# Stores of the last batch from SP's and ScalarE's queues, a three-part store as three operations, and a new order of all engines

## The chip, the cores and the metric

The kernel runs on one core of a Trainium2 chip. The metric is the device time of one execution in microseconds (us). The engines are PE (TensorE, matrix products), VectorE (DVE), ScalarE (ACT), GpSimd (POOL) and SyncE (SP). Each works through its own list of instructions in order and waits on semaphores for the others. DMAs are issued from the lists of SP, POOL and, after the change, ScalarE.

## The reference

Attention over blocks mixed by a Sinkhorn-normalized matrix, then a Fourier mix and a feed-forward layer, over 4 batches, 768 tokens and 8 heads of 64 (so 512 columns):

```python
for _ in range(5):
    P = P - np.max(P, axis=-1, keepdims=True)
    P = np.exp(P)
    P = P / (np.sum(P, axis=-1, keepdims=True) + 1e-09)
    P = P / (np.sum(P, axis=-2, keepdims=True) + 1e-09)
k_sorted = np.einsum('bhij,bhjcd->bhicd', P, k_b)
v_sorted = np.einsum('bhij,bhjcd->bhicd', P, v_b)
scores = scale * np.matmul(q_b, k_sb.transpose(0, 1, 2, 4, 3))
attn = softmax(scores);  x = attn @ v_sb      # x: (4, 768, 512)
...
mixed = np.real(fft(fft(x, axis=1), axis=2))
u = x + mixed
un = (u - mu) / np.sqrt(var + 1e-06)
ch = np.maximum(un @ w_ch1, 0.0) @ w_ch2      # 512 -> 2048 -> 512
out = u + ch                                  # float32
```

## The kernel before

The 768 tokens of a batch are handled as six tiles of 128 rows. `TOK` lists the tokens of each: tiles T = 0, 1, 2 hold tokens 1 to 383 and token 0 at the end of T = 2, tiles T = 3, 4, 5 the mirrored tokens downward from 767. A row of T = 0, 1 lies beside the next one in the output, so those tiles are stored by one plain DMA. T = 2 is stored in three parts: 112 rows, 15 rows and the single row of token 0. T = 3, 4, 5 run backwards in the output and are stored by POOL with an indirect DMA over a table of row numbers (`rows`, line 1627).

Per batch the work is: block mixing of k and v (`kq`, `vmix`), transposes of q, scores, exponentials on ScalarE (line 1268), subtraction of 1 (`em1`, line 1281 on VectorE or 1283 on ScalarE), the product with v (`av`, line 1298), the division (line 1315), two DFT steps (`dft1`, `dft2`), the normalization (square, logarithm L1534, exponential, `un`), a transpose (`uT`, `utev`), and the feed-forward layer. For batches 0 and 1 its first product is `ff1` (line 1592). For batches 2 and 3 `ff1_seven` (from line 1698 on) builds the product from seven smaller ones: VectorE forms the differences E1, a second one in place, E2 and E4 of the inputs (operations tagged `es`, line 1716); the products (line 1728) collect in banks A, D and Q; ScalarE copies A out (line 1743), VectorE adds (line 1736). The second product in batches 1 to 3 is `ff2_chunk` (line 1779 on), one chunk per pair of tiles (t, t + 3), again with sums on VectorE (line 1796), products of 8 matmuls (line 1820), a copy by ScalarE (`p1`, line 1851) and additions into u by VectorE (line 1837). A chunk's last product is `p3`; the addition behind it completes the tile T = t, which is then stored. In batch 3 the chunks are planned in the order t = 2, 0, 1, and the last one, t = 1, stores its tile in two halves of 256 columns: the left half after `p2`, the right one after `p3`.

What is issued, and in which order, is written out by hand. `P.add` collects operations, numbered in the order in which they are added, each with the engines that may do it, its cost on each, its function, what it reads and writes, and a tag. `ORDER` holds for each engine the list of these numbers. `schedule` goes through the five lists, gives out buffers and returns the order in which the instructions are emitted; it does not change the lists. An operation that names two engines is done by the one in whose list it stands. The tool that makes dependencies would order all stores to `out` behind one another; `declare_no_dep` says which pairs write different rows.

`store` (line 1609) is one operation per tile. For T = 2 it issues all three parts on SP. Its cost says SP for T < 3 and POOL for T > 2. The engine lists hold 461 (PE), 347 (ACT), 568 (DVE), 70 (POOL) and 61 (SP) numbers. In batch 3 these numbers matter below: 1331 and 1345 are products with E2, 1324 makes E2; 1488 is the first product of chunk t = 1, whose bank ScalarE copies; 1460, 1481 and 1503 are the last products (`p3`) of the chunks t = 2, 0 and 1; 1461, 1482 and 1504 the additions behind them; 1462, 1483, 1502 and 1505 the stores of T = 2, T = 0 and of the two halves of T = 1; 1498 is the addition before POOL's last store (1499, T = 4). Before the first `ff1`: 272, 275 and 278 are `un`, 273, 276 and 279 the transposes, 274, 277 and 280 the copies of those into `ut`; 394 is an attention product. The numbers are those of the kernel before; after the change all from 1463 on are higher by 2.

PE works in several kinds of matmul (full tile, halves, quarters); `MODE` and `TURN` are the planner's notion of what a change from one kind to the next costs.

Of the kernel before, what the change touches and what calls it, by code (L numbers as in the profile page):

```python
# [22 lines left out]
DM = 512  # L23
# [44 lines left out]
    ),  # L68
    "ACT": (
# [425 lines left out]
def kernel(  # L495
# [10 lines left out]
    nc = tc.nc  # L506
# [9 lines left out]
    P = Plan()  # L516
# [99 lines left out]
    def load(dst, src, nbytes, w, prio, eng="POOL", r=(), after=(), gone=()):  # L616
# [10 lines left out]
          tag="spin")  # L627
# [78 lines left out]
    for n in range(2):  # L706
# [8 lines left out]
          prio=-9100.0, tag="small")  # L715
# [76 lines left out]
    def ptb():  # L792
# [5 lines left out]
        tag="pk")  # L798
# [1233 lines left out]
```

## Time and profile before

| | before |
|---|---|
| median of 3 runs | 255.49 us (255.2 to 255.81) |
| the profiled execution | 255.66 us |
| its span, first to last instruction | 253.5 us |
| granted TensorE clock, mean | 0.996 |
| PE, VectorE, ScalarE, POOL busy | 96%, 89%, 62%, 22% |
| DMA packets | 42775, 26.51 MB |

Times inside the profile run from the span's start. A line of the instructions in order of time gives start and duration in us, the engine, the line of the kernel, the operation and its tiles; in brackets stands the engine's idle time before it and what ended it. SPq is SP's queue: the time there is the issue of a DMA, not its transfer. A line of the busy times by stage gives from:to, the length, and for each engine the busy time with the number of instructions.

### The profile page before, as it was taken

What the parts mean: (1) busy time and instruction counts of PE and PEld (TensorE: products, weight loads), DVE (VectorE), ACT (ScalarE), POOL (GpSimd) and SP (SyncE); (2) the same over time, 40 slices, a digit from 0 to 9 for tenths busy, and PEclk for the clock granted to TensorE, in tenths of its full rate; (3) what the DMA queues carried; (4) which work ended last, traced back from release to release, by engine and by line L of the source; (5) the groups of instructions that cost most, each with busy time, mean ns of one, the idle gap of its engine ahead of it and who ended that gap; (6) DMA issues with size and microseconds to landing.
All of it is one profiled execution on the core that took longest, in us unless ns stands there. A gap on an engine that the chain in (4) does not pass through costs nothing.

```text
span 253.5 us, 7235 instructions
## 1 busy us (share of the span) xinstructions
PE 244.3 (96%) x2895; PEld 167.5 (66%) x2895; DVE 226.0 (89%) x604; ACT 157.3 (62%) x372; POOL 56.2 (22%) x86
## 2 busy tenths in 40 slices
PE   4999999999999999999999999999999999999992
PEld 1347775676665666654667658887667887667882
DVE  4699999999999788989999999998889987799892
ACT  4159999999753779645886685524699425563000
POOL 8955322243359000012100000021100000310031
PEclk9999999999999999999999999999999999999998
DMA  6999999999999933033412003232202410410025
GB/s 129 206 211 314 210 214 217 208 207 184 140 133 158 189 18 75 0 79 101 83 27 48 0 5 70 50 106 83 83 3 43 65 21 0 168 43 3 0 83 207
DMA packets 42775, 26.51 MB, mean 105 GB/s; under 512 B 30202, under 2 KB 39176, under 8 KB 42740
## 3 DMA queue, kind: packets, MB, share of 16 engines
q0 software_dynamic: 23632, 18.35, 43.5%
q1 hardware_dynamic: 19110, 7.71, 15.7%
q8 instruction: 22, 0.36, 0.6%
q14 instruction: 11, 0.09, 0.1%
HBM read 29.07 MB, written 6.29 MB: 139 GB/s over the span
## 4 chain that ended last, share of the span: by engine, by line
PE 87%; DMA 5%; DVE 5%; issue 1%; POOL 1%; ACT 0%; DVEq 0%; POOLq 0%
PE bank L1820 17%; PE bank L1592 17%; PE bank L1728 14%; PE bank L1649 8%; PE bank L1298 5%; DMA kq<-in_k_dram 5%; PE bank L961 4%; PE bank L1259 3%; PE bank L1463 3%; PE bank L1372 3%; DVE u L1837 3%; PE bank L1192 1%; PE bank L1467 1%; PE bank L967 1%; PE bank L1228 1%; PE bank L1063 1%
## 5 line engine op out<-in xcount | busy, mean ns | idle before, releaser
L1592 PE MATMUL bank<-ut,w1sb 128*128 128x384 f16 x256 | 47.6, 326 | 0.0
L1268 ACT ACTIVATE ex<-bank 96x384 f32<-96x384 f32 x64 | 28.7, 486 | 11.2 <-PE bank L1451 5.6
L1627 POOL DMA_INDIRECT out_dram<-u,rows x9 | 9.8, 1094 | 114.8 <-DVE u L1837 79.2
L1743 ACT COPY vsf<-bank 128x384 f32<-128x384 f32 x48 | 21.5, 483 | 22.1 <-PE bank L1728 21.7
L1592 PEld LDWEIGHTS <-w1sb 128*128 128x128 f16 x256 | 23.5, 97 | 14.6 <-issue 0.3
L1820 PEld LDWEIGHTS <-hr 128*128 128x128 f16 x288 | 28.2, 98 | 4.3
L1736 DVE CUSTOM_DVE_ANT_0 hr<-bank,vsf 128x384 f16<-128x384 f32 x48 | 24.9, 551 | 3.1 <-PE bank L1728 2.2
L1649 PE MATMUL bank<-w2sb,hr 128*128 128x512 f16 x96 | 23.7, 379 | 0.0
L1820 PEld LDWEIGHTS <-vcx 128*128 128x128 f16 x216 | 21.1, 98 | 3.3
L1604 ACT ACTIVATE hr<-bank 128x384 f16<-128x384 f32 x41 | 19.4, 489 | 4.4 <-PE bank L1592 4.2
L1728 PE MATMUL bank<-ut,w1sb 128*128 128x384 f16 x96 | 20.9, 326 | 0.0
L1820 PE MATMUL bank<-w2sb,hr 128*128 128x256 f16 x144 | 18.2, 273 | 0.0
L1820 PE MATMUL bank<-kq,vcx 128*128 128x256 f16 x144 | 18.0, 273 | 0.0
L1298 PEld LDWEIGHTS <-eb 97*128 97x128 f16 x416 | 15.7, 98 | 3.4 <-issue 0.7
L1298 PE MATMUL bank<-vsf,eb 97*128 97x65 f16 x416 | 17.4, 193 | 0.2
L1728 PEld LDWEIGHTS <-w1sb 128*128 128x128 f16 x128 | 12.5, 98 | 7.4
L619 POOL DMA_DIRECT2D kq<-in_q_dram x18 | 15.5, 875 | 8.1 <-PE bank L1451 2.1
L1315 DVE TENSOR_TENSOR rt<-bank,rz 128x384 f16<-128x384 f32 x32 | 16.9, 547 | 0.2
L1281 DVE TENSOR_SCALAR eb<-ex 96x384 f16<-96x384 f32 x46 | 15.9, 359 | 1.2 <-ACT ex L1268 1.1
L862 ACT CAST vsf<-bank 96x512 f16<-96x512 f32 x20 | 12.9, 681 | 5.4 <-PE bank L961 5.3
L862 ACT CAST ks<-bank 128x384 f16<-128x384 f32 x24 | 10.6, 486 | 6.5 <-PE bank L1192 5.0
L1522 ACT ACTIVATE ex<-u,mv 128x512 f16<-128x512 f32 x18 | 13.0, 724 | 1.9 <-DVE mv L1514 1.6
(202 smaller groups left out, 531.5 us busy)
## 6 DMA issues: line engine op xcount, KB each, us to landing
w1sb<-in_moe_w_ch_dram POOLq DMA_DIRECT2D x4, 512.0 KB, 20.4
w2sb<-in_moe_w_ch_dram POOLq DMA_DIRECT2D x4, 512.0 KB, 22.1
hr<-in_v_dram POOLq DMA_DIRECT2D x2, 768.0 KB, 9.3
kq<-in_v_dram POOLq DMA_DIRECT2D x2, 768.0 KB, 16.6
kq<-in_k_dram POOLq DMA_DIRECT2D x8, 192.0 KB, 6.6
kq<-in_q_dram POOLq DMA_DIRECT2D x16, 96.0 KB, 6.5
out_dram<-u SPq DMA_DIRECT2D x5, 256.0 KB
kq<-in_k_dram POOLq DMA_DIRECT2D x2, 384.0 KB, 10.1
```

The lines of the kernel that those rows point to most:

```text
L862: (nc.scalar.copy if e == "ACT" else V.tensor_copy)(dst, src)
L1268: nc.scalar.activation(ex.ap[0:96], pss[h2].ap[0:96, 0:384], AF.Exp, scale=SCALE),
L1281: V.tensor_scalar(ed, src, -1.0, None, op0=ALU.add)
L1298: nc.tensor.matmul(po.ap[:, 65 * T:65 * T + 65], eb.ap[:, e0:e0 + 128], vsf[0:97, vi:vi + 65], start=(n == 0), stop=(n == len(WIN[T]) - 1) ...
L1315: P.add({"DVE": (0.465, 0.56)}, lambda _: V.tensor_tensor(rt.ap[:, :, D * h:D * h + D], po3()[:, :, 0:D], rz.ap[:, :, None].broadcast_to([ ...
L1592: nc.tensor.matmul(ps.ap[:, 0:GT], w1sb[:, c, 128 * fc:128 * fc + 128], ut.ap[:, c, :], start=(c == 0), stop=(c == 3))
L1604: nc.scalar.activation(hr[g][:, fc, :], ps.ap[:, 0:GT], AF.Relu)
L1649: nc.tensor.matmul(ps.ap, hr[g][:, fc, 128 * tt:128 * tt + 128], w2sb[:, fc, :], start=(fc == 0), stop=(fc == 15))
L1728: nc.tensor.matmul(ps.ap[:, 0:GT], lhs[:, c, fi], rhs()[:, c, :], start=(start and c == 0), stop=(c == 1), skip_group_check=True)
L1736: return P.add({"DVE": (0.47, 0.57)}, lambda _: V._custom_dve(TENSOR_ADD_SAT, out=hr[g][:, fc, :], in0=p.ap[:, 0:GT], in1=o.ap, s0=FMAX, s ...
L1743: P.add({"ACT": act(GT)}, lambda _: nc.scalar.copy(x.ap, A.ap[:, 0:GT]), r=[A], w=[x], prio=pr_v - 1, tag="pc", after=avs)
L1820: nc.tensor.matmul(ps.ap[:, o:o + 256], lhs()[:, fc], rhs[:, fc], start=(start and fc == 0), stop=(fc == 7), skip_group_check=True)
```

## The change

Three things change.

- In batch 3 the tiles T = 0, 1, 2 are stored through operations that SP or ScalarE may issue, whichever list holds them. T = 2's three parts become three operations (1462, 1463 and 1464 in the new numbering).
- The pairs of stores that are free of order are kept in one more list (`late`, for the stores issued by ScalarE).
- The lists of PE, ScalarE and VectorE are written anew, those of POOL and SP in part. 95 operations change their engine: 44 from ScalarE to VectorE, 50 from VectorE to ScalarE, and one store (the left half of T = 1, 1502 before) from SP to ScalarE, where the two new parts of T = 2 also stand. The lists of PE and POOL hold the same operations as before.

At the end of the lists the new order has, in the old numbers: PE ... 1473 1470 1488 1493 1460 1500 1481 1503; VectorE ... 1495 1496 1453 1497 1474 1461 1498 1501 1482 1504; ScalarE 1489, the single row of T = 2, 1502, the 15 rows of T = 2; SP ... 1321 1300 1279, the 112 rows of T = 2, 1483, 1505. Before, PE ended with 1500 1491 1493 1481 1449 1503 1460, VectorE with 1482 1501 1498 1453 1504 1461, ScalarE with 1489, and SP with 1321 1300 1483 1502 1279 1505 1462.

```diff
 ORDER = {
     "PE": (
...
-        "1436 1434 1448 1469 1450 1471 1473 1452 1451 1492 1467 1472 1488 "
-        "1470 1490 1500 1491 1493 1481 1449 1503 1460 "
+        "1298 1471 1448 1420 1446 1451 1452 1450 1473 1492 1469 1494 1474 "
+        "1493 1449 1475 1472 1490 1495 1460 1502 1483 1505 "
     ),
     "ACT": (
...
-        "1390 1412 1430 1416 1407 1418 1432 1435 1393 1421 1447 1468 1489 "
+        "1390 1365 1404 1426 1412 1393 1430 1416 1432 1418 1435 1447 1407 "
+        "1421 1470 1491 1464 1504 1463 "
     ),
     "DVE": (
...
-        "1478 1495 1487 1479 1474 1441 1494 1445 1496 1497 1482 1501 1498 "
-        "1453 1504 1461 "
+        "1441 1457 1445 1478 1458 1496 1468 1479 1489 1480 1481 1497 1498 "
+        "1453 1499 1476 1461 1500 1503 1484 1506 "
     ),
...
     "SP": (
-        "12 13 14 15 17 228 231 230 229 16 584 598 415 416 626 418 417 612 "
-        "937 943 691 677 949 524 719 526 528 705 574 575 549 576 573 553 551 "
-        "795 825 827 799 820 828 797 826 822 824 1092 1113 1134 870 874 895 "
-        "872 899 897 1321 1300 1483 1502 1279 1505 1462 "
+        "12 13 14 15 16 230 231 228 229 415 416 417 584 17 598 626 418 612 "
+        "937 691 943 949 677 705 524 528 526 719 576 574 573 575 549 551 553 "
+        "827 828 825 795 799 797 820 826 1092 822 824 1113 1134 870 872 895 "
+        "874 899 897 1321 1300 1279 1462 1485 1507 "
     ),
 }
...
     def store(b, T, u, pr_v, half=None):
+        if b == 3 and T < 3:
+            m = slice(0, DM) if half is None else slice(half, half + 256)
+            for lo, hi in ((0, 112), (112, 127), (127, 128)) if T == 2 else (
+                    (0, 128),):
+                def f(e, lo=lo, hi=hi):
+                    t0 = TOK[T][lo]
+                    x = (nc.sync if e == "SP" else nc.scalar).dma_start(
+                        out[b, t0:t0 + hi - lo, m], u.ap[lo:hi, m])
+                    same, other = ((direct, late) if e == "SP" else
+                                   (late, direct))
+                    for y in stores + other:
+                        tc.declare_no_dep(x.ins, y.ins,
+                                          reason="each row stored once")
+                    same.append(x)
+                P.add({"SP": (0.58 if hi - lo > 99 else 0.45, 2.8),
+                       "ACT": (0.5, 2.9)}, f,
+                      r=[(u, "l") if half == 0 else (u, 1)], w=[], prio=pr_v,
+                      tag="out")
+            return
+
         def f(_):
...
-                for y in stores if T < 3 else stores + direct:
+                for y in stores + late if T < 3 else stores + direct + late:
...
-    goal, stores, direct, lastp = [], [], [], []
+    goal, stores, direct, late, lastp = [], [], [], [], []
```

169 rows, old and new, of the table ORDER are left out of this document.

## The prediction

> **What bounds the kernel now.** I read the page first, then the busy times by stage, then the instructions in order of time in the last 15 us.
>
> ```profile
> span 253.5 us, 7235 instructions
> PE 244.3 (96%) x2895; PEld 167.5 (66%) x2895; DVE 226.0 (89%) x604; ACT 157.3 (62%) x372; POOL 56.2 (22%) x86
> PE 87%; DMA 5%; DVE 5%; issue 1%; POOL 1%; ACT 0%; DVEq 0%; POOLq 0%
> ```
> ```profile
> 15.00:20.00 5.00, 4.74 (x98) 3.12 (x94) 4.86 (x17) 4.69 (x11) 2.04 (x3) 1.00 1.27 253
> 25.00:30.00 5.00, 4.84 (x106) 3.82 (x107) 4.97 (x14) 4.88 (x12) 2.09 (x4) 1.00 1.31 203
> 45.00:50.00 5.00, 4.99 (x70) 3.37 (x64) 4.87 (x18) 4.91 (x14) 1.45 (x2) 1.00 1.10 208
> 55.00:150.00 95.00, 95.00 (x1355) 59.37 (x1354) 87.92 (x241) 66.81 (x164) 18.36 (x26) 1.00 0.72 87
> 150.00:249.00 99.00, 99.00 (x780) 76.01 (x778) 89.12 (x204) 47.95 (x114) 10.38 (x17) 1.00 0.21 57
> ```
>
> After the length stand the busy times of PE, weight loads, VectorE (DVE), ScalarE (ACT) and POOL, then clock, DMA share and GB/s. From 55 to 249 us PE is never without work: 95.00 of 95 and 99.00 of 99, at clock 1.00. There an order can gain only by fewer matmul turns, and loses wherever PE has to wait. From 15 to 50 us VectorE and ScalarE are both full (4.7 to 5.0 of 5) and PE has its few gaps. The third place is the tail, where no engine computes:
>
> ```profile
> 241.24 0.37 ACT L1851 COPY ex<-bank 128x256 f32<-128x256 f32 x1 [1.37 <-PE bank L1820]
> ...
> 246.53 0.75 DVE L1837 TENSOR_TENSOR u<-bank,u 128x256 f32<-128x256 f32 x2
> ...
> 247.15 1.91 PE L1820 MATMUL bank<-w2sb,vcx 128*128 128x256 f16 x16
> 247.20 0.68 DVE L1837 TENSOR_TENSOR u<-u,ex 128x512 f32<-128x512 f32 x1
> ...
> 248.16 0.96 POOL L1627 DMA_INDIRECT out_dram<-u,rows  x1 [2.45 <-DVE u L1837]
> 248.68 0.33 SPq L1614 DMA_DIRECT2D out_dram<-u  x1
> 249.10 0.42 DVE L1837 TENSOR_TENSOR u<-bank,u 128x256 f32<-128x256 f32 x1 [0.45 <-issue]
> 249.55 0.33 SPq L1619 DMA_DIRECT2D out_dram<-u  x1
> 249.93 0.43 SPq L1621 DMA_DIRECT2D out_dram<-u  x1
> 250.42 0.47 SPq L1623 DMA_DIRECT2D out_dram<-u  x1
> ```
>
> PE ends at 247.15 + 1.91 = 249.06. The last VectorE addition, T=2's, waits for it and ends at 249.52. SP then issues the three parts one behind the other, until 250.89; the span ends 2.6 us later. So the kernel ends 4.44 us after PE.
>
> **The sum's base.** The profiled execution took 255.66 us, 2.16 outside the span and 0.17 above the median of 255.49. I sum on the former and take 0.17 off at the end.
>
> **1. The tail.** T=2's last product (1460) moves from last to fourth from last on PE, and its addition (1461) to fifth from last on VectorE. Last on both is now T=1's right half, one store on SP. After PE: addition 0.42, one issue of 0.33 to 0.37 (the half stores of line 1614), the same 2.6: 249.06 + 0.04 + 0.42 + 0.03 + 0.35 + 2.6 = 252.5 against 253.5. Two issues and their gaps, 250.89 - 249.88 = 1.01 us, leave the path.
>
> What could take their place? On ScalarE's queue the order is: last copy, T=2's single row, T=1's left half, T=2's 15 rows. The first waits for T=2's addition; behind it no computation is queued, only stores whose data come later still. ScalarE issues no DMA in this trace, so I bound its issue by SP's for such parts; the third row is one product in the chain of waits:
>
> ```profile
> L1621 SPq DMA_DIRECT2D out_dram<-eb x1: 747/747/747, 217.3 to 217.3; - x1
> L1623 SPq DMA_DIRECT2D out_dram<-u x3: 237/247/471, 98.1 to 250.4; - x3
> 229.75 0.87 PE bank L1820 x8
> ```
>
> A product of this stage is 0.87 us, an addition 0.75 / 2 = 0.38 or 0.68. T=2's product is done 3 x 0.87 = 2.6 us before PE ends. VectorE's list sets the rest: its last wait for ScalarE's copy (0.37, L1851) follows product 1488, 5 x 0.87 = 4.4 before PE's end, and ten operations come after it, T=2's addition the sixth. So that ends about 4.4 - 0.4 - 6 x 0.38 = 1.7 before PE's end, the left half's 0.68 + 0.38 later, 0.6 before, and the ninth 0.3 before: the tenth, which waits for PE's end, finds VectorE free by 0.3 us. Without that cover the end would slip by what is lacking. On ScalarE, two issues of 0.24 to 0.75 after the left half's addition end between 0.1 before and 0.9 after PE's end; SP's last ends 0.85 after. The dear end costs 0.05; I take nothing, as stores of 15 rows or more took 0.33 to 0.47 in the tail.
>
> The same 16 engines must carry the bytes, though:
>
> ```profile
> 248.00:249.00 1.00, 1.00 (x10) 0.70 (x8) 0.64 (x2) 0.00 (x0) 0.84 (x1) 1.00 1.02 366
> 249.00:250.00 1.00, 0.06 (x1) 0.00 (x0) 0.42 (x1) 0.00 (x0) 0.12 (x1) 1.00 0.98 347
> 250.00:251.00 1.00, 0.00 (x0) 0.00 (x0) 0.00 (x0) 0.00 (x0) 0.00 (x0) 1.00 1.01 346
> 251.00:252.00 1.00, 0.00 (x0) 0.00 (x0) 0.00 (x0) 0.00 (x0) 0.00 (x0) 0.79 0.59 191
> ```
>
> The DMA share (second last column) is 1.0 for three microseconds and 0.59 of the fourth: transfers end near 251.6, 2.5 after PE. From T=2's addition on the new order stores 224 + 30 + 2 + 256 + 128 + 128 KB and POOL's 256 KB: 1024 KB, at 350 GB/s 3.0 us. I put their start 1 us after that addition (which ends 2.2 to 1.7 before PE), an estimate out of the 2.6 us that lie between the last issue and the end of the span, so they end 1.8 to 2.3 after PE against 2.5 now. By issues the gain is 1.0, by transfers alone 0.2 to 0.7. POOL's last store, issued at 248.16 now, waits for the operation after T=2's addition and moves by less than half a microsecond; it is in these bytes. I take 0.9, nearer the issues, because the last one issued before is a single 2 KB row that waits for few of those bytes. Bounds: 0.2 to 1.1.
>
> The Trainium skill, DMA: Bandwidth & Descriptors, Rules for kernel authors, says that spreading DMAs over SP, ScalarE and GpSimd brings no bandwidth and saves only the issue time, since all run on the same 16 engines. By that rule alone the gain is the transfers' (the second rival's time); the shares of 1.0 agree that the engines are full, but no run so far shows two such queues.
>
> **2. The first stage.** Up to the first feed-forward product (L1592) PE only fills gaps:
>
> ```profile
> 50.08 0.30 ACT L1534 ACTIVATE ny<-mv,eps 128x3 f32<-128x3 f32 x1
> 53.32 0.42 DVE L862 COPY ut<-bank 128x512 f16<-128x512 f16 x1
> 53.53 0.57 PE L1298 MATMUL bank<-vsf,eb 97*128 97x65 f16 x13
> 53.95 1.30 PE L1592 MATMUL bank<-ut,w1sb 128*128 128x384 f16 x7
> 63.27 0.40 PE bank L1298 x13
> 73.28 0.86 PE bank L1649 x4
> 74.65 0.97 PE bank L1649 x4
> ```
>
> (The first four rows are instructions in order of time, the last three pieces of the chain of waits.) The new order sets one attention product (394, L1298, 0.40) behind that point and has 71 changes between kinds of matmul instead of 73; one costs 0.97 - 0.86 = 0.11, so 0.2 in all. If the first product starts at 53.95 again, PE ends 0.40 - 0.2 = 0.2 later. When can it start? VectorE has 132 operations ahead of its first normalization (272) instead of 137, at (4.86 + 4.97 + 4.87) / 49 = 0.30 us each 1.5 less; ScalarE has 82 ahead of the logarithm (L1534) instead of 81, at (4.69 + 4.88 + 4.91) / 37 = 0.39 more. Start: 1.5 earlier to 0.4 later. I take 0.4 earlier, near the middle: the stage is worth -0.2, with -1.3 to +0.6 as bounds. Of the 94 computing operations that change engine, 44 go to VectorE and 50 to ScalarE; after 55 us ScalarE's idle 28 of 95 us cover them.
>
> SP's list changes there too: three moves of rows for batch 1 (415 to 417) come before two transposes of queries (584, 598) read only by batch 2's scores, which PE's list has behind the first feed-forward products. Costed at nothing; that cover gone, batch 2's scores are delayed by what the transposes are late.
>
> **3. The opening of batch 3.** Two second-layer products of batch 2 more than before are put behind 1331, the first user of E2, VectorE's third difference (operation 1324):
>
> ```profile
> 207.89 0.55 DVE L1716 TENSOR_TENSOR qt<-ut,qt 128x768 f16<-128x768 f16 x1
> 209.51 0.81 PE L1728 MATMUL bank<-qt,kq 128*128 128x384 f16 x4
> 205.00:210.00 5.00, 5.00 (x45) 4.23 (x44) 4.38 (x10) 0.98 (x3) 0.00 (x0) 1.00 0.00 0
> ```
>
> E2 is ready at 208.44, first used (1345) at 209.51; 1331 follows 0.33 later, at 209.84. PE now comes to it 2 x 0.87 = 1.74 earlier, at 208.1, and would wait 0.34. VectorE, with 485 operations ahead instead of 490 and 0.62 us idle in these five, can be earlier. I take +0.2, bounds 0 to 1.7.
>
> **The sum**: 255.66 - 0.9 - 0.2 + 0.2 - 0.17 = **254.6 us**.
>
> **The rivals.** *The order gains too.* Both full engines reach the first stage's end 1.3 early and E2 is in time: 254.6 - 1.1 - 0.2 = 253.3. For it: five VectorE operations fewer. Against it: ScalarE's one more, on an engine at 4.7 to 5.0 of 5. *The transfers set the end.* The tail gives 0.4 instead of 0.9: 255.1. For it: the shares of 1.0. Against it: two parts were issued after most bytes were under way. *ScalarE's queue is slow.* The second queue then does not shorten the end as it should: if its last store lands 0.8 us after SP's, the time is 255.4. The trace has no such store, for or against. *PE waits at batch 3*, the other side. The sum of 190 to 210 us shows how full VectorE is there:
>
> ```profile
> sum 20.00, PE 20.00 PEld 16.39 DVE 18.56 ACT 10.64 POOL 0.00; mean PE 5.00 PEld 4.10 DVE 4.64 ACT 2.66 POOL 0.00
> ```
>
> VectorE works 18.56 of the 20. If E2 comes as late as the old order could bear, at 209.84, while PE is there at 208.1, the wait is 1.74 instead of 0.2: 256.1. It decides from a wait of 1.6 on, which gives 256.0; against it stand VectorE's idle 0.62 and its shorter list.
>
> **How the numbers follow.** 0.2% of 255.49, about what a measurement of this kernel can tell from no change, is 0.5: faster is below 255.0, slower above 256.0. Forecast 0.47, with its own range of 254.0 to 255.2 (0.42 faster, 0.05 same); order gains 0.15, faster; transfers 0.17 (0.05 faster, 0.12 same); slow queue 0.06 (0.04 same, 0.02 slower); PE waits 0.15, slower. That makes 0.62, 0.21 and 0.17. The range runs from 253.5 to 256.1: it leaves out about half of the best and half of the worst case.
>
> **What would show it.** Right: one SP issue after the last addition, ScalarE's three before it, the span ending about 3.5 us after PE, PE full from 55 us on and ending within 0.5 us of 249.06. Wrong: a DMA share of 1.0 that lasts until 1.9 us before the end (the transfers), a store of ScalarE landing last (its queue), or idle PE before L1728 near 208 us (batch 3). A PE end more than 0.7 us from 249.06 would prove my reading of the order wrong whatever the total.

## The result and the profile after

The changed kernel takes 256.81 us (median of 6 runs, 256.43 to 257.55) against 255.56 (6 runs, 255.05 to 255.81) in the same job, that is, the same session of measurement: the ratio is 1.0055, with a 95% interval of 1.0037 to 1.0073. It is 1.25 us slower where 0.9 us faster was forecast, and lies above the range of 253.5 to 256.1.

The profiled execution took 256.64 us, with a span of 254.9. Its page:

```profile
span 254.9 us, 7245 instructions
PE 243.6 (96%) x2896; PEld 167.7 (66%) x2896; DVE 225.2 (88%) x598; ACT 159.5 (63%) x378; POOL 56.7 (22%) x86
```

PE is busy 0.7 us less than before and the span is 1.4 us longer. The busy times by stretch (length, then PE, weight loads, VectorE, ScalarE, POOL, clock, DMA share, GB/s) say where:

```profile
15.00:20.00 5.00, 4.68 (x82) 2.85 (x78) 4.78 (x16) 4.50 (x11) 1.83 (x3) 1.00 1.27 254
25.00:30.00 5.00, 4.67 (x100) 3.60 (x97) 4.97 (x13) 4.81 (x12) 2.00 (x4) 1.00 1.31 204
55.00:150.00 95.00, 94.78 (x1363) 59.66 (x1362) 86.00 (x232) 68.42 (x167) 18.19 (x26) 1.00 0.71 87
150.00:249.00 99.00, 99.00 (x778) 75.90 (x779) 90.07 (x213) 48.76 (x117) 9.58 (x16) 1.00 0.19 55
249.00:250.00 1.00, 0.89 (x9) 0.55 (x6) 0.55 (x3) 0.00 (x0) 0.95 (x1) 1.00 0.74 228
250.00:251.00 1.00, 0.00 (x0) 0.00 (x0) 0.35 (x1) 0.00 (x0) 0.01 (x1) 1.00 0.99 347
251.00:252.00 1.00, 0.00 (x0) 0.00 (x0) 0.00 (x0) 0.00 (x0) 0.00 (x0) 1.00 0.97 329
252.00:253.00 1.00, 0.00 (x0) 0.00 (x0) 0.00 (x0) 0.00 (x0) 0.00 (x0) 0.53 0.41 142
```

PE is busy for less of the first stage (4.68 and 4.67 where before had 4.74 and 4.84), is full from 150 to 249 us, so the opening of batch 3 costs nothing, and has 0.2 us of idle time in the middle, where before had none. PE's last rows and the stores, in order of time:

```profile
247.98 1.91 PE L1840 MATMUL bank<-w2sb,vcx 128*128 128x256 f16 x16
...
248.20 2.51 SPq L1616 DMA_DIRECT2D out_dram<-u  x3
248.20 1.85 ACTq L1616 DMA_DIRECT2D out_dram<-u  x3
248.69 0.78 DVE L1857 TENSOR_TENSOR u<-bank,u 128x256 f32<-128x256 f32 x2
249.05 0.96 POOL L1647 DMA_INDIRECT out_dram<-u,rows  x1 [2.21 <-DVE u L1857]
249.92 0.42 DVE L1857 TENSOR_TENSOR u<-bank,u 128x256 f32<-128x256 f32 x1 [0.45 <-PE bank L1840]
```

PE ends at 247.98 + 1.91 = 249.89, 0.83 later than before (249.06). The last addition ends at 250.34 and SP issues one store behind it, as the change intends; yet the span ends 5.0 us after PE instead of 4.4. What ends it stands in no row of computing work. It is among the instructions of the kernel's last line, each with the shortest, median and longest of its group in ns, and the first and last start. Before:

```profile
L2027 POOLq DRAIN  x3: 46/97/4655, 247.9 to 253.3; - x3
L2027 SPq DRAIN  x3: 7/7/13, 252.7 to 253.0; - x3
```

and the changed kernel:

```profile
L2047 POOLq DRAIN  x3: 46/97/5272, 248.8 to 254.6; - x3
L2047 SPq DRAIN  x3: 7/7/13, 253.4 to 254.3; - x3
```

SP's first DRAIN comes when all its waits for landed stores are over: 252.7 before, 253.4 after. POOL's long one begins behind its last store's issue and ends at 247.9 + 4.66 = 252.6 before, at 248.8 + 5.27 = 254.1 after. The span ends about 0.8 us behind the later of the two. Before, they were 0.1 to 0.2 us apart, SP's last; after, POOL is last by 0.65. POOL's own list is the same in both kernels but for the numbering, so when its last store starts is set by the lists of the engines that it waits for.

In the middle, VectorE writes a tile u late, and PE waits for VectorE:

```profile
124.53 0.69 DVE L1490 SCALAR_TENSOR_TENSOR u<-rt,bank 128x510 f32<-128x510 f16 x1 [0.38 <-PE bank L1156]
```
```profile
124.43 0.82 PE L1592 MATMUL bank<-ut,w1sb 128*128 128x384 f16 x4
125.48 0.56 PE L1298 MATMUL bank<-vsf,eb 97*128 97x65 f16 x13 [0.23 <-DVE u L1501]
125.88 0.81 PE L1592 MATMUL bank<-ut,w1sb 128*128 128x384 f16 x4
126.53 0.56 PE L1298 MATMUL bank<-vsf,eb 97*128 97x65 f16 x13
```

The rows of PE overlap where one product follows another at once: four ff1 products and the start of the next take 126.53 - 125.88 = 0.65 us there, but 125.48 - 124.43 = 1.05 at the wait. So the wait costs PE 0.40 us, though only 0.23 of it shows as idle time.

Together these say where PE's 0.83 us go. Its first ff1 product starts at 53.95 before and here at

```profile
53.98 0.81 PE L1592 MATMUL bank<-ut,w1sb 128*128 128x384 f16 x4
```

From there to its end PE takes 249.06 - 53.95 = 195.11 us before and 249.89 - 53.98 = 195.91 after, 0.80 more: 0.40 for the attention product that now stands behind that point, and 0.40 for the wait. This stretch is a finer measure than the medians: the traces of e3, e5 and e8 below, which keep the order of before up to the last products, give 195.11 as well, while their first ff1 product starts anywhere from 53.5 to 54.2.

So three places are to be explained: the first stage, 124 us, and the tail.

### The profile page after: what moved, and what is told of

Read it like the earlier page. It is cut to its first block, busy times and chain, and to the rows that moved or that the text cites. A ratio compares the mean times of both kernels' runs of the same rounds, so it can differ in the third digit from the quotient of the medians.

```text
span 254.9 us, 7245 instructions
## 1 busy us (share of the span) xinstructions
PE 243.6 (96%) x2896; PEld 167.7 (66%) x2896; DVE 225.2 (88%) x598; ACT 159.5 (63%) x378; POOL 56.7 (22%) x86
## 4 chain that ended last, share of the span: by engine, by line
PE 89%; DMA 4%; DVE 3%; issue 1%; POOL 0%; ACT 0%; DVEq 0%; POOLq 0%
PE bank L1840 22%; PE bank L1592 17%; PE bank L1748 14%; PE bank L1669 8%; PE bank L1298 5%; DMA hr<-in_v_dram 4%; PE bank L1259 3%; PE bank L1463 3%; PE bank L1372 3%; PE bank L961 3%; PE bank L1467 1%; PE bank L880 1%; PE bank L1192 1%; PE bank L1228 1%; PE bank L1063 1%; PE bank L967 1%
## 5 line engine op out<-in xcount | busy, mean ns | idle before, releaser
L1592 PE MATMUL bank<-ut,w1sb 128*128 128x384 f16 x256 | 48.3, 326 | 0.0
L1647 POOL DMA_INDIRECT out_dram<-u,rows x9 | 9.1, 1007 | 103.6 <-DVE u L1857 56.2
L1748 PE MATMUL bank<-ut,w1sb 128*128 128x384 f16 x96 | 21.5, 326 | 0.0
L1871 ACT COPY ex<-bank 128x256 f32<-128x256 f32 x9 | 3.4, 373 | 26.6 <-PE bank L1840 26.5
L1281 DVE TENSOR_SCALAR eb<-ex 96x384 f16<-96x384 f32 x42 | 14.5, 355 | 1.8 <-ACT ex L1268 1.5
L1647 POOL DMA_INDIRECT out_dram<-eb,rows x3 | 3.7, 1229 | 52.2 <-DVE eb L1857 52.0
```

Of the source, the lines that this page charges most:

```text
L1281: V.tensor_scalar(ed, src, -1.0, None, op0=ALU.add)
L1592: nc.tensor.matmul(ps.ap[:, 0:GT], w1sb[:, c, 128 * fc:128 * fc + 128], ut.ap[:, c, :], start=(c == 0), stop=(c == 3))
L1748: nc.tensor.matmul(ps.ap[:, 0:GT], lhs[:, c, fi], rhs()[:, c, :], start=(start and c == 0), stop=(c == 1), skip_group_check=True)
```

## The experiments

Operation numbers are those of before (in the changed kernel's lists, all from 1463 on are two higher). "Before" is timed again in each job, at a median of 255.55 to 255.63. PE's end is read from each trace; the tail is the span less that.

**First look at the tail: e1 to e4.** e1 takes before's lists up to what starts at 228 us and the changed ones behind it; e2 the changed lists up to 200 us and before's behind. PE's lists at the two cuts:

```diff
 e1, against before
-1431 1411 1428 1420 1394 1408 1446 1422 1436 1434 1448
+1431 1411 1408 1394 1428 1434 1436 1422 1469 1448 1420
 e2, against the changed kernel
-1307 1268 1267 1266 1286 1269 1289 1284 1277 1340
+1307 1268 1286 1290 1288 1269 1289 1284 1309 1305
```

> The order of before up to 228 us, then the changed kernel's last batch: its stores on two queues and its order of the last additions. Three theories of the 4.98 us that the changed kernel needs after its last matmul (before: 4.44). (a) SP's issues end the kernel, as the prediction had it: PE ends at 249.1 as before, one issue behind the last addition instead of three, so 0.9 us faster than before, 254.7. (b) POOL ends it: its last store is issued 0.9 us later than before (249.05 against 248.16) and lands more slowly (3.79 us against 3.19), and POOL's closing DRAIN ends 1.24 us behind the landing: PE ends at 249.1, the DRAIN near 253.3, the span near 254.1, so 0.3 to 0.6 us slower than before, 255.9 to 256.2. (c) The tail is not the cause at all and the whole loss is TensorE's: within 0.2 us of before. In every theory PE's end does not move; if it is later by 0.3 us or more, the tail's own order costs TensorE time and that part has to be taken off first.

> The complement of e1: the changed kernel's order up to 200 us, then the order and the single-queue stores of before. If the loss is two separate parts, 0.8 us of TensorE before 126 us and 0.5 us of tail, PE ends at 249.8 to 249.9, the span ends 4.4 to 4.5 us behind it, and the kernel is 0.6 to 0.9 us slower than before, near 256.3; with e1 the two differences add up to the 1.25 us of the change within 0.4 us. If the order of the first 200 us costs nothing by itself and only the tail does, it is within 0.2 us of before.

e1 took 257.36 us (ratio 1.0061 to 1.0085), e2 257.52 (1.0068 to 1.0094): both slower than the changed kernel, which no theory had. Both lists were cut where they don't fit together. PE's waits in e1 at 226 to 232 us, and in e2 at 196 to 204:

```profile
PE bank L1748 <- DVE hr L1756: 0.9, 1, 0.9
```
```profile
PE bank L1840 <- DVE hr L1816: 1.0, 1, 1.0
```

The times of e1 and e2 thus say nothing; only e1's tail does: PE ends at 250.26, the span 4.9 us later, as long as in the changed kernel.

e3 moves one addition on VectorE in before, that of POOL's last store:

```diff
-1482 1501 1498 1453 1504 1461
+1482 1501 1453 1504 1461 1498
```

> Before, with one step moved: VectorE makes the addition for POOL's last store (T=4 of the last batch) last, behind the one for T=2, so that it ends near 250.2 instead of 247.88; nothing of SP's stores, of TensorE or of the queues changes. (a) SP's three issues behind the T=2 addition end the kernel: 0 to 0.1 us, the store has room. (b) The landing of POOL's store ends it, without a drain behind it: it lands near 253.4 to 253.7, 1.0 to 1.3 us behind SP's last landing of before, so about 1.0 us slower. (c) POOL's DRAIN ends it, 1.24 us behind the landing: near 254.7 to 254.9 with the closing 0.77 us behind it, so 1.7 to 2.2 us slower, 257.3 to 257.8.

257.26 us, 1.7 slower than before (1.0057 to 1.0083): (c). PE ends at 249.08 and SP's issues are unchanged:

```profile
249.57 0.33 SPq L1618 DMA_DIRECT2D out_dram<-u  x1
249.95 0.43 SPq L1620 DMA_DIRECT2D out_dram<-u  x1
250.42 0.96 POOL L1626 DMA_INDIRECT out_dram<-u,rows  x1 [4.70 <-DVE u L1836]
250.43 0.24 SPq L1622 DMA_DIRECT2D out_dram<-u  x1
```
```profile
L2026 POOLq DRAIN  x3: 46/97/4176, 250.2 to 254.9; - x3
```
```profile
out_dram<-u,rows POOLq DMA_INDIRECT x1, 2.7
```

The store, issued at 250.42, landed 2.7 us later, at 253.1; the DRAIN ended at 250.2 + 4.2 = 254.4, 1.2 us behind the landing, and the span at 255.1. POOL's last store alone, made late, sets the end, with 2 us behind its landing.

e4 is e1 with that store made early:

```diff
 PE
-1491 1449 1473 1470 1488 1493 1460 1500 1481 1503
+1491 1473 1488 1493 1449 1470 1460 1500 1481 1503
 VectorE
-1495 1496 1453 1497 1474 1461 1498 1501 1482 1504
+1495 1496 1497 1498 1453 1474 1461 1501 1482 1504
```

> e1 with POOL's last store made earlier: TensorE makes the three products that T=4's tile still needs ahead of T=2's and T=0's (1473, 1488, 1493 ahead of 1449), and VectorE its three last additions ahead of T=2's (1496 to 1498 ahead of 1453). Two queues for SP's stores as in the changed kernel. (b, POOL's store and DRAIN end the changed kernel): the store is issued near 246.5 and its DRAIN ends by 251.5, so that SP's and ScalarE's landings end the kernel: one issue behind the last addition and 3.5 to 4.0 us from PE's end to the span's, so 0.4 to 0.9 us faster than before, 254.7 to 255.2. (c, the end is set by when all the bytes have moved, in whatever order): no better than e1, 0.3 to 0.6 us slower than before. If PE's end moves by more than 0.3 us, the new order of products costs by itself.

257.00 us. The tail fell to 3.3 us, but 1493 now waited 1.0 us for a bank that VectorE had not emptied, beside e1's wait, and PE ended at 251.55:

```profile
PE bank L1840 <- DVE ex L1857: 1.0, 1, 1.0
```

**The tail without those waits: e5 to e8.** e5 cuts behind the last ff1 product of before (1434) instead:

```diff
-1434 1448 1469 1450 1471 1473 1452 1451 1492 1467 1472 1488 1470 1490 1500 1491 1493 1481 1449 1503 1460
+1434 1469 1448 1451 1452 1450 1471 1490 1467 1492 1472 1491 1449 1473 1470 1488 1493 1460 1500 1481 1503
```

> e1 again without its seam: the whole ff1 part of the last batch in the order of before, and only the products, additions and stores behind it in the changed order. e1 spoiled its own comparison, since a relu stood out of place and TensorE lost 1.1 us at 229 us. If the drain of POOL ends the changed kernel, whose store is late: PE ends at 249.1, the span 4.7 to 5.0 us behind it, 0.2 to 0.6 us slower than before, 255.8 to 256.2. If SP's issues end it: the span 3.5 us behind PE, 0.9 us faster, 254.7.

256.18 us, 0.5 slower than before (1.0008 to 1.0029). PE ends at 249.32 and the tail is 5.0 us. POOL's DRAIN is over at 248.3 + 5.2 = 253.5, 0.7 us behind SP's waits:

```profile
L2047 POOLq DRAIN  x3: 46/97/5244, 248.3 to 254.0; - x3
L2047 SPq DRAIN  x3: 7/7/13, 252.8 to 253.8; - x3
```

So the changed tail costs 0.5 us by itself; the single issue behind the last addition brings nothing that can be seen.

e6 is e5 with e4's early store and a product between 1488 and 1493 that hides most of the wait:

```diff
-1491 1449 1473 1470 1488 1493 1460 1500 1481 1503
+1491 1473 1488 1449 1493 1470 1460 1500 1481 1503
```

> e5 with POOL's last store earlier, this time without e4's wait for a bank: products in the order 1473 1488 1449 1493 1470, VectorE's 1496 to 1498 ahead of 1453. Theory (POOL's store and drain end the changed kernel): PE ends at 249.1, the store is issued 1.5 to 2 us earlier than in e5, POOL's drain is over before SP's last landing, and the span ends 3.4 to 3.6 us behind PE as in e4 (3.35): 0.8 to 1.1 us faster than before, 254.5 to 254.8. If the bytes set the end: as e5.

e7 puts e6's direct stores all on SP:

```diff
 SP
-1279 1462(112 rows) 1483 1505
+1279 1462(112 rows, 15 rows, 1 row) 1502 1483 1505
 ScalarE
-1489 1462(1 row) 1502 1462(15 rows)
+1489
```

> e6 with all stores on SP: T=2's three parts, then T=1's left half, T=0, T=1's right half; ScalarE issues none. What the second queue is worth when POOL is out of the way. If the order of the additions does the work and not the queue: T=2's three issues are over by 249.5 and the last issue still follows the last addition at once, so within 0.2 us of e6. If the second queue does it: 0.4 to 0.9 us slower than e6.

e6 took 255.70 us, 0.5 less than e5 and level with before (0.999 to 1.0012); e7 255.49 (0.9984 to 1.0006), 0.2 less still. The tails are 4.2 us each. In e6:

```profile
L2047 POOLq DRAIN  x3: 46/97/4821, 246.3 to 252.8; - x3
L2047 SPq DRAIN  x3: 7/7/13, 252.3 to 252.6; - x3
```
```profile
249.00:250.00 1.00, 0.00 (x0) 0.00 (x0) 0.37 (x1) 0.00 (x0) 0.00 (x0) 1.00 0.90 302
250.00:251.00 1.00, 0.00 (x0) 0.00 (x0) 0.00 (x0) 0.00 (x0) 0.00 (x0) 1.00 0.91 322
251.00:252.00 1.00, 0.00 (x0) 0.00 (x0) 0.00 (x0) 0.00 (x0) 0.00 (x0) 1.00 0.32 108
```

POOL's DRAIN is over at 251.1 and SP's waits end the kernel, at 252.3; the expected 3.4 to 3.6 us came out at 4.2. In e4, where PE's waits had let most bytes go out earlier, the tail was 3.3: with POOL out of the way, the stores of the last three microseconds are next. The second queue is worth nothing here, or less.

e8 changes before in one point: 112 rows of T=2's tile on SP, the single row and the 15 rows on ScalarE.

```diff
 SP
-1483 1502 1279 1505 1462
+1483 1502 1279 1505 1462(112 rows)
 ScalarE
-1468 1489
+1468 1489 1462(1 row) 1462(15 rows)
```

> Before, in its own order, with only the three parts of T=2's tile on two queues: 112 rows on SP, the single row and the 15 rows on ScalarE. SP then has one issue behind the last addition instead of three, and ScalarE two beside it. If the issues end the kernel (the prediction): 0.4 to 0.9 us faster. If POOL's drain, which ended at 252.57 in before against 252.77 of SP's waits, takes over at once: 0 to 0.2 us faster and no more.

255.40 us, 0.2 faster than before (0.998 to 1.0002): not told apart from no change, and clearly not 0.4 to 0.9. PE ends at 248.62 in this trace, 0.44 earlier than before, because its first ff1 product starts 0.44 earlier, ahead of anything that the edit touches. The tail is 4.4 us, as before. POOL is last now, at 247.5 + 4.76 = 252.3:

```profile
L2046 POOLq DRAIN  x3: 46/97/4760, 247.5 to 252.8; - x3
L2046 SPq DRAIN  x3: 7/7/13, 252.1 to 252.5; - x3
```
```profile
246.71 1.91 PE L1839 MATMUL bank<-w2sb,vcx 128*128 128x256 f16 x16
...
248.24 1.21 SPq L1615 DMA_DIRECT2D out_dram<-u  x2
...
249.12 0.92 ACTq L1615 DMA_DIRECT2D out_dram<-u  x2
```

SP's last issue ends 0.83 us behind PE's end, where before had 250.89 - 249.06 = 1.83, and ScalarE's 1.42. Yet SP's waits are over 252.1 - 248.62 = 3.5 us behind PE's end against 252.7 - 249.06 = 3.6. So the last issue comes 1.0 us earlier on SP and 0.4 earlier on either queue, and the waits for the landings end only 0.1 to 0.2 earlier.

**124 us and the first stage: e9 to e12.** e9 swaps two products of the changed kernel.

```diff
-716 1010 730 1008 736
+716 1010 1008 730 736
```

> The changed kernel with one swap on TensorE: the ff1 product 1008 ahead of the av product 730, so that TensorE has 0.65 us of work while 730 waits at 124.4 to 125.5 us for a bank that VectorE empties. If that wait, 0.40 us in the changed kernel's trace and absent before, is worth its length at the end: PE ends at 249.5 instead of 249.89 and the kernel is 0.4 us faster than the changed one (256.81), 256.4. If a later wait swallows it: within 0.15 us of the changed kernel. If the wait only moves behind 1008: the same, with the wait seen at its new place.

257.10 us (1.0046 to 1.0073), no faster than the changed kernel. The wait moved behind 1008, to a discrete Fourier product (L1372), and the view of VectorE's waits from 117 to 130 us names another releaser than the changed kernel's trace did:

```profile
DVE rz L1312 <- PE bank L1298: 0.5, 1, 0.5
DVE u L1490 <- DMA out_dram<-u,rows: 0.3, 1, 0.3
```

VectorE waits for the landing of POOL's last store of batch 0, which still reads the tile that it is to write. (In the changed kernel's trace the landing and product L1156 ended within 0.1 us of each other, and the view names the later.)

e10 is the changed order for what starts in the first 53.9 us, with before's behind it.

```diff
 PE, against before
-0 77 69 78 91 73 79 137 121 ... 394 279 397 276 377 400 1506 922 902
+0 77 69 78 73 79 91 121 137 ... 397 279 276 361 400 394 1506 922 902
```

> The changed kernel's order of all engines for what starts in the first 53.9 us, av 394 ahead of the first ff1 as in before, and the order and stores of before for the rest. What the reordered first stage does by itself. The prediction: 0.2 us faster. Theory from the two traces: the waits at 14 to 22 us cost more than those that went, the same products are done 0.3 to 0.6 us later: PE ends at 249.4 to 249.7, 0.3 to 0.6 us slower than before, 255.9 to 256.2. If it comes out within 0.15 us of before, the loss of the changed kernel is not in this stage.

260.12 us (1.0168 to 1.0198), by another bad cut: the first ff1 product starts at 57.5 instead of 53.95. It shows nothing of the first stage. e11 is the changed kernel with e6's moves (its diff, and e4's on VectorE):

> The changed kernel with POOL's last store earlier, by e6's moves alone (products 1473 1488 1449 1493 1470, VectorE's 1496 to 1498 ahead of 1453). If POOL's store and drain end the changed kernel: the tail behind PE's end goes from 4.98 to 4.1 to 4.3 us as in e6, PE's end is later by the 0.3 us for which 1493 waits for its bank, so 0.4 to 0.6 us faster than the changed kernel, 256.2 to 256.4. If not: no faster than 256.7.

256.44 us, 0.37 less than the changed kernel (256.81, in another job), just short of the 0.4 to 0.6 expected: the tail is 4.2 us, and 0.3 goes in 1493's wait. e12 is e11 with e9's swap and with before's lists for the first 53.9 us:

```diff
 PE, against e11
-0 77 69 78 73 79 91 121 137 ... 397 279 276 361 400 1506 906 916 394
+0 77 69 78 91 73 79 137 121 ... 394 279 397 276 377 400 1506 906 916
```

> All three mends in one: the first 53.9 us in the order of before, then the changed order with e9's swap and e11's early store of POOL. If the loss of the changed kernel is those three places (0.5 + 0.4 + 0.5 us, of which 0.3 comes back as 1493's wait), the changed order's two saved turns of TensorE are left and the tail of e6: PE ends at 249.0 to 249.2, the span near 253.2, 255.2 to 255.6, equal to before or faster by up to 0.3 us. If something else costs, it stays 0.4 us or more slower than before.

255.94 us (1.0003 to 1.002), above the 255.2 to 255.6 expected: better than e11 by 0.5, and still 0.3 behind before, with 0.5 us of waits at 126 us left, since the swap does not work.

**What holds the tile, and the first stage again: e13 to e17.** e13 (changed kernel), e16 (before) and e17 (changed kernel) move the store or the transpose beside it:

```diff
 e13, PE, then VectorE
-996 692 997 697
+996 997 692 697
-566 532 533 998
+566 998 532 533
 e16, VectorE
-567 998 758 1035 533
+567 758 1035 998 533
 e17, PE
-692 997 697 683
+692 697 997 683
```

> The changed kernel with batch 0's last store by POOL earlier: VectorE's addition 998 ahead of 532 and 533, and TensorE's score product 692 behind 997, on which 998 waits. e9 showed that the 0.4 us wait at 124 us follows POOL's store: VectorE writes a tile u that this store still reads, issued at 120.30 and landed at 124.47, and the banks that TensorE needs are emptied behind that write. Theory (the landing of POOL's store delays VectorE): the store is issued 0.4 us earlier, VectorE does not wait, TensorE's wait at 124 to 127 us goes, PE's end is 0.4 us earlier, 256.4. Rival (the order of the work around it costs the time): the wait stays or appears elsewhere, within 0.15 us of the changed kernel.

> Before with one addition moved, the reverse of e13: 998 behind 758 and 1035 on VectorE, so that batch 0's last store by POOL is issued 1.0 us later (near 121.0). In before the store lands just as VectorE comes to the tile (124.25 and 124.31). If its landing delays VectorE: VectorE waits 0.9 to 1.0 us at 124.3, and TensorE some of that, 0.4 to 1.0 us slower than before. If the landing does not matter: within 0.15 us.

> The changed kernel with one move on TensorE: the score product 697 ahead of the feed-forward product 997. e13 and e16 refuted that the issue of batch 0's last store decides when it lands: in e13 it was issued earlier beside the work around it and landed 4.7 us later, in e16 a full 1.3 us later than in before and landed at the same time. In all four traces its packets run last, behind those of SP's transpose of queries (L1211), which waits for the score product that frees its tile. New theory (the transpose holds the store, the store holds VectorE's tile): the transpose is issued 0.7 to 0.9 us earlier, the store lands at 123.7 or before, VectorE has no wait at 124 us, TensorE's 0.4 us go and the kernel takes 256.4. If 697 or 683 waits for a bank at its new place, as 683 did in e13, that wait (0.2 to 0.7 us) stands against the gain; the transpose, the landing and VectorE's wait are then to be read by themselves. Rival (VectorE's wait is not for the landing): the wait at 124 us stays though the store has landed.

e13 took 257.83 us (1.0065 to 1.0105), e17 257.75 (1.0053 to 1.0102), e16 256.50 (1.0023 to 1.0052). All three lost time to waits that the edit itself made: 683 for ScalarE's exponentials in e13 (0.6 us), 697 in e17 (1.0, for something that the view does not name), a relu for its product in e16 (0.9). Their times don't decide; the landings do. POOL's store of batch 0, issue, us until landing, and the start of VectorE's write of the tile:

| kernel | issued | to landing | landed | tile written | transpose issued |
|---|---|---|---|---|---|
| before | 119.97 | 4.3 | 124.3 | 124.31 | 119.26 |
| changed | 120.30 | 4.1 | 124.4 | 124.53 | 119.64 |
| e9 | 120.56 | 4.1 | 124.7 | 124.71 | 119.89 |
| e13 | 120.43 | 5.4 | 125.8 | 125.89 | 120.70 |
| e16 | 121.29 | 2.8 | 124.1 | 124.64 | 118.97 |
| e17 | 121.89 | 3.4 | 125.3 | 125.57 | 119.95 |

The row of e13 (5.4, not the 4.7 that stands in e17's expectation), and that of e16:

```profile
out_dram<-u,rows POOLq DMA_INDIRECT x1, 5.4
```
```profile
out_dram<-u,rows POOLq DMA_INDIRECT x1, 2.8
```

The write never starts ahead of the landing, and in four of six follows it within 0.2 us: that VectorE waits for the landing is shown. What sets the landing is not the issue: e16's store, issued 1.3 us later than that of before, landed earlier. It took longest where SP's transpose was issued just behind it (e13, 5.4, and 5.3 in e14 and e15, which hold the same move) and least where the transpose had been issued over 2 us ahead (e16, 2.8). That the transpose holds the store up fits all six, but no run moved the transpose alone without a wait of its own, and e17 did not bring it forward at all (119.95 against 119.64); this part stays open.

Nor does the landing alone cost PE time. In e3, which has before's order here, VectorE's view names the same wait:

```profile
DVE u L1489 <- DMA out_dram<-u,rows: 0.3, 1, 0.3
```

PE loses nothing by it: from its first ff1 product to its end it takes 195.11 us as in before. In the changed order PE's product 730 stands where it needs the bank that VectorE empties behind this write. So it takes the landing and the new order around it, and no run tells how the 0.40 us would divide.

e14 joins e13 and e11; e15 is e14 with before's first 53.9 us (e12's diff).

> The changed kernel with e13's and e11's moves: batch 0's last store and batch 3's last store by POOL both earlier. If the two add up (0.4 and the 0.37 that e11 measured): 256.0. Against before (255.6) what is left is the first stage, 0.4 us.

> e14 with the order of before in the first 53.9 us, av 394 ahead of the first ff1. The difference from e14 is what the reordered first stage costs. By the two traces (first ff1 no earlier, one av more behind it, 0.2 us of turns saved): 0.3 to 0.5 us faster than e14, 255.5 to 255.7, level with before. If the first stage costs nothing: equal to e14 within 0.15 us.

e14 took 256.89 us (1.0045 to 1.0077), e15 256.37 (1.002 to 1.0045). e13's move costs rather than gains, so the levels missed, but the two differ in the first stage alone: it costs the changed order 0.52 us. From the first ff1 product to PE's end the traces of e14 and e15 differ by 0.45 us, about the 0.40 of the attention product that the new order sets behind that point. e11 and e12 differ by 0.50, the swap included.

**In search of a version faster than both: e18**, e7 with the wait for the bank removed.

```diff
 PE
-1473 1488 1449 1493 1470 1460
+1473 1488 1449 1470 1493 1460
 VectorE
-1496 1497 1498 1453 1474
+1496 1453 1497 1498 1474
```

> The candidate to beat both kernels: e7 (order of before until the last batch's ff1 part, then the changed tail with POOL's last store early and all direct stores on SP) with the product 1470 ahead of 1493 and VectorE's 1497 and 1498 behind 1453, so that the 0.33 us for which 1493 waited for its bank go. If that wait was on the path: PE ends 0.3 us earlier than in e7, T=2's three issues 0.5 earlier, POOL's drain stays ahead of SP's last landing: 0.3 to 0.5 us faster than e7, 255.0 to 255.2, 0.4 to 0.6 faster than before. If the bytes of the last three microseconds set the end: as e7, 255.4 to 255.5.

255.44 us (0.9971 to 1.0005), as e7 and not the 0.3 to 0.5 faster that was expected. The tail is still 4.1 us. In the trace the gain is there: PE's wait is gone, and from the first ff1 product to the span's end it takes 199.2 us against 199.6 in e7 and in before; the medians do not tell it from no change. No version was found that beats before by more than the measurement can tell.

## Why the prediction was wrong, step by step

**The tail, -0.9: it cost 0.5** (e5). The step that failed is the reading of before's end: "SP then issues the three parts one behind the other, until 250.89; the span ends 2.6 us later." The 2.6 us were taken as what follows SP's last issue, whatever else happens. But POOL's path ended only 0.1 to 0.2 us ahead of SP's, so no shortening of SP's alone could bring more than about 0.2. And the landings follow the issues only in part: e8, which only takes issues off SP's queue, ends the last issue 0.4 us earlier and the waits 0.1 to 0.2 earlier, and its span ends as long behind PE as before (its median is 0.2 lower, which is not told apart from no change). POOL's last store was counted in the bytes and not as an end of its own. Measured from PE's end its issue hardly moved, 249.89 - 249.05 = 0.84 us ahead of it against 249.06 - 248.16 = 0.90; what moved is its landing, 3.8 us after the issue in e5 against 3.2 in before, among T=2's, T=0's and T=1's stores that now all come in the same two microseconds. That these stores slowed it is read from the rows and was not tried by itself.

Beneath that the second assumption was wrong too. "I take 0.9, nearer the issues": with POOL's store early, e6 and e7 have a tail 0.2 to 0.3 shorter than before. That is the low end of what was given for the transfers (0.2 to 0.7), a rival with a chance of 0.17. The rule that was weighed there (the Trainium skill, DMA: Bandwidth & Descriptors, Rules for kernel authors: more issuing engines bring no bandwidth) was the better guide: e7, with one queue, is no slower than e6 with two, 255.49 against 255.70. The sign named for that rival, a DMA share of 1.0 until 1.9 us before the end, was not seen in the changed kernel (the share falls at 252, 2.9 before the end), since POOL's DRAIN lay behind it.

**The first stage, -0.2: it cost 0.5** (e14 against e15). The term was -0.4 + 0.40 - 0.2: an earlier start, the av product behind the first ff1, two saved turns. Only the 0.40 was right. The 0.2 for the turns does not show: the stretch from the first ff1 on is longer by 0.80 us, as much as the av product and the wait at 124 us make without any turn saved. One turn was priced from two rows of the chain of waits (0.97 and 0.86); whether the price or the count of turns was off stays open. The step that failed most is "I take 0.4 earlier", from the number of operations ahead on VectorE and ScalarE. The first ff1 product starts at 53.98 against 53.95, though the first product that waits for input had come 0.24 us earlier (8.94 against 9.18). Leaving e10 aside, the seven traces with the changed first stage give 53.88 to 54.52 and the twelve with before's 53.48 to 54.26: no earlier. Fewer operations did not help; waits stand in their place, as in these rows of the changed kernel:

```profile
14.08 0.69 DVE L812 TENSOR_TENSOR bdk<-bank,pack 128x512 f16<-128x512 f32 x1 [0.58 <-ACT tkh L821]
...
17.54 0.53 PE L1228 MATMUL bank<-pack,kq 128*64 128x128 f16 x12 [0.32 <-DVE bdk L812]
```

VectorE has one copy less (tkh, moved to ScalarE) and waits 0.58 us for it. That this wait is the cause is read from the rows and was not tried.

**The opening of batch 3, +0.2: 0.** PE is full from 150 to 249 us. The rival that ended slower (a wait of PE at batch 3, chance 0.15) had the right direction in the wrong place.

**Not costed: 0.4 at 124 us.** VectorE's write had no slack before: the store landed at 124.3 and the tile was written at 124.31. PE had some, as e3 shows; in the new order the wait reaches PE. The prediction said that a new order loses wherever PE has to wait, and looked for such a place only where PE's list passes an operation of VectorE. This wait comes through a tile that a store still reads.

Together, in the two profiles: 0.03 (first ff1) + 0.40 (av product) + 0.40 (124 us) + 0.5 (tail) = 1.3 us; their spans differ by 1.4 as printed, the medians of the times by 1.25. The prediction's own test, a PE end more than 0.7 us from 249.06, came out at 0.83: the order was misread, and the tail as well.

## What to carry to other kernels

Ahead of shortening the chain that ends last, write down the end of every other engine's chain, closing instructions and landings included: here POOL's ended only 0.1 to 0.2 us ahead of SP's, so the edit could gain about 0.2 at most, and making POOL's last store 2.3 us later cost 1.7 (e3). A store is an operation on the buffer that it reads until it lands; in a new order, check for each reused buffer that the landing still comes before the next write. And to measure part of a reordering, cut the lists where a stage ends on all engines: e1, e2, e4 and e10 each lost 0.9 us or more at the cut.

## What was not expected of the hardware

- POOL's closing DRAIN ended 1.2 us behind the landing of its last indirect store (e3: 254.4 against 253.1), and some 0.8 us more passed to the span's end. In all 20 traces, early store or late, it is 1.24 us. The Trainium skill, VectorE: DVE Perf Modes, The DRAIN you can't avoid, puts the DRAINs of a kernel's beginning and end at about 12 ns on all engines. SP's agree with 7 to 13 ns; POOL's longest, 4176 to 5272 ns, does not, nor do the longest of PE (2155) and VectorE (464) in before.
- POOL's indirect stores of one tile took 2.7 to 5.9 us from issue to landing. What sets this was not isolated; the longest in the table above have a transpose issued just behind them.
- The time outside the span was 2.05 to 2.2 us (median of each kernel's runs) in before and in the kernels with before's order behind the first stage, and 1.77 to 1.82 in the changed kernel and all others with its order there, e12 and e15 too, whose first stage is that of before. So 0.3 us of the longer span does not reach the time. Nothing in the profile shows why.
